# One division for logits and outputs, no rests behind batch 0's scatters, batch 2 in batch 0's rows, and a new written order

## The chip, the cores and the metric

The kernel runs on one core of a Trainium2 chip. The metric is the device time of one execution in microseconds (us); smaller is better. The engines are TensorE (PE; its weight loads are listed apart as PEld), VectorE (DVE), ScalarE (ACT), GpSimd (POOL) and SyncE (SP, which only starts DMA transfers here). Each takes its own instructions in the order in which they are written.

## What is computed

Attention with a polynomial sketch of the keys and queries, then a layer of eight experts of which every token goes to one. B = 4, H = 4, S = 1088, D = 32, R = 8; 4352 tokens of 128 elements, E = 8, F = 1024; everything in fp32.

```python
def phi(x):                                    # S1, S2: (8, 32)
    a = np.einsum('rd,bhsd->bhsr', S1, x)
    b = np.einsum('rd,bhsd->bhsr', S2, x)
    return np.einsum('bhsi,bhsj->bhsij', a, b).reshape(*x.shape[:-1], 64)
q_p, k_p = phi(q), phi(k)
kv = np.einsum('bhsf,bhsd->bhfd', k_p, v)
z = np.sum(k_p, axis=2)
num = np.einsum('bhsf,bhfd->bhsd', q_p, kv)
den = np.einsum('bhsf,bhf->bhs', q_p, z)[..., None] + 1e-06
x = (num / den).transpose(0, 2, 1, 3).reshape(4352, 128)

logits = x @ w_gate                            # (4352, 8)
expert_idx = np.argmax(logits, axis=1)
probs = softmax(logits)                        # with 1e-9 added to the sum
for e in range(8):
    mask = expert_idx == e
    out[mask] = probs[mask, e, None] * (np.maximum(x[mask] @ w1[e], 0) @ w2[e])
```

## The kernel before

The schedule is written by hand. Every piece of work is a named operation (`@op(name)`), and `ORDER`, a table of some 1,100 names, says in which order they are emitted. An engine's queue is what of this list falls to it, so that an operation that waits holds back all that stands behind it on its engine. Buffers are taken from rings and given back in the same order.

**Attention.** Names are `k{b}{c}` and `q{b}{c}` for batch b and half c (512 tokens), `kr{r}` and `qr{r}` for what is left over of two batches (64 tokens each, handled as one batch). `L.*` are loads on SP. PE transposes the inputs (`.t`), ACT copies them out of the matmul banks (`.x`), PE applies the sketch (`.a`), ACT copies one factor (`.l`), DVE forms the products (`.s`, `.o`: L442, L455, 128x1024 elements). For keys PE then adds up kv (`.v`); `e{b}.*` finish it. For queries each half again has two turns: PE transposes phi(q) (`.T`, `.U`; L566), ACT copies it (`.c`, `.d`), PE forms the numerators, the denominator and, by a folded gate matrix, the logits of each head in one product (`.n`, `.N`; L584). ACT adds 1e-6 to the denominators (`.p`, L596), DVE inverts them (`.e`, L600), multiplies the logits (`.g`, L604, into `lgh`) and the outputs (`.y`, L611, into a buffer of the ring `flat`), and ACT copies the outputs with their 16-bit halves apart into the token rows `x_rows` (`.f`, L617). A trailing 2 marks the second turn.

**Routing.** `r{b}` on a batch: DVE adds the heads' logits and takes the greatest (`.a`), ACT the exponentials (`.x`), DVE the one-hot `oh` of the expert (`.b`, L667 to L672) and the gate's weight (`.c`), PE ranks the tokens of each expert (`.p`, L686 and L688), DVE turns ranks into row numbers `row_i` (`.d`, L695 to L701), and POOL scatters the token tiles, 128 tokens each, to their experts' rows in DRAM (`.s{u}`, L707: eight for even and nine for odd batches). Behind every scatter stands `breathe()`, which issues by turns no and two small memsets of `fill` (L632). A token's own number stands in the last word of its row; POOL writes these numbers once per batch (`number_rows`, L236).

**Experts.** The rows are worked on in tiles of 128 tokens of one expert: `j0` to `j9` once batches 0 and 1 are scattered, `j10` to `j17` after batch 2, `j18` to `j26` after batch 3, and the split tiles `j27` to `j37` of twice 64 tokens with two experts (`j34` on lie in conditional blocks `m0`, `m1`; of the four, two are executed). `t0` to `t3` are DVE's tables of which tile belongs to which expert. Per tile: SP loads the rows transposed (`.l`, L897, and the gate with the token number, L899; split tiles take rows, `xr`, and transpose on PE, L948), ACT undoes the 16-bit interleaving (`.c`, L958), DVE copies the expert's w1 out of the eight into `wide` (`.w`, `.W`, L966), PE multiplies by w1 in two halves (`.u`, `.U`; L980, split L984), ACT and DVE apply the maximum with 0 (`.r` into hTa on ACT, L1004; `.q` into hTb on ACT for `j0` to `j9`, L1011, else on DVE, L1013), PE multiplies by w2 (`.d`; L1025, split L1029), ACT scales by the gate (`.y`, L1042), and POOL scatters the rows to the output (`.s`, L1047, with `breathe()` behind). `.X` is ACT's copy of w2 for split tiles (L973).

The first load of a group waits for all scatters of the batches that it needs:

```python
                for b in range(min(g + 2, B)):
                    for i in scattered[b]:
                        tc.add_manual_dep(d.ins, i.name, landed, reason="rows of the tile")
```

Of the kernel before, what the change touches and what calls it, by code (L numbers as in the profile page):

```python
# [13 lines left out]
U16 = mybir.dt.uint16  # L14
# [8 lines left out]
warm L.q0 k00.t k00.x S.t L.q1 k01.t S.m k01.x k00.a k01.a L.k1 k00.l k00.s kr0.t kr0.x L.v1 k00.o kr0.a k00.v  # L23
k01.l k01.s kr0.l k01.o q01.t kr0.s q00.t q01.x k01.v e0.s kr0.o e0.r q00.x q11.t C.late e0.k L.qr0 q00.a L.fill
q00.l q11.x e1.s C.later L.x7 q01.a q00.s q00.o q01.l L.kr1 e0.t q01.s q01.o e0.m e0.z k10.t L.k2 q11.a L.k3
k10.x q10.t k11.t k10.a q10.x q01.U q11.l q11.s q00.T k11.x qr0.t q10.a q11.o e0.c k11.a k10.l L.q2 k10.s qr0.x
k10.o q00.c k11.l D0 k11.s q01.d q00.U q00.d q01.T k11.o qr0.a L.qr1 q00.n q00.N q10.l q10.s q00.p L.x0 q01.N
q01.c q01.n q00.p2 q00.e q00.e2 q00.y2 q00.f2 q01.p q00.y L.vr1 k10.v qr0.l k11.v q01.e q01.p2 q01.g q10.o
q01.e2 e1.r qr0.s k20.t e1.k q00.g q01.g2 kr1.t qr0.o q00.g2 r0.a r0.b k31.t q10.U q10.T k20.x k30.t kr1.x r0.x
q10.d qr0.T L.q3 qr0.c k20.a r0.p r0.c k31.x k30.x r0.d q11.U q01.y k20.l kr1.a q11.d k20.s e1.t q00.f e1.c e1.m  # L30
k21.t r0.s2 e1.z q01.y2 kr1.l kr1.s q11.T r0.s1 q01.f k31.a q11.N q01.f2 r0.s4 qr0.n k21.x k20.o qr0.p L.v2 L.w7
r0.s0 kr1.o q10.N q11.p2 qr0.e qr0.y k31.l k30.a k31.s k21.a q10.p2 qr0.g k30.l q10.e2 q11.c q11.e2 k20.v q10.y2
# [40 lines left out]
def kernel(  # L73
# [12 lines left out]
    nc = tc.nc  # L86
# [66 lines left out]
    flat_bufs = ring("flat", 3, [128, 2, DM])  # L153
# [987 lines left out]
```

## Time and profile before

| what | value |
|---|---|
| median of three runs | 214.54 us (213.92 to 215.52) |
| profiled execution | 212.96 us, of which the span of the engines is 211.2 us |
| granted clock of TensorE, mean | 0.974 of full |
| PE busy | 191.7 us, 91% of the span |
| DVE, ACT, POOL busy | 126.4, 104.2, 95.1 us |
| bytes moved by DMA | 23.22 MB, mean 110 GB/s |

Line numbers (L617) are those of the kernel before. A row of a group gives line, engine, operation, output and inputs with their shapes, the count, and behind the bars the busy us, the mean ns of one, and how long the engine sat idle just before and what ended most of it. A row of a timeline gives start, duration, instruction and count; in brackets, the idle time before it and what released it ("issue": nothing that the trace shows). A "q" behind an engine's name means its sequencer. A row of the chain is a piece of the work that ended last, followed back from the end. In all of them, the releaser is inferred from the semaphore that came last.

### The profile page before, as it was taken

Reading aid. Unit: us, or ns where it says so; the run is one execution under the profiler, and the core shown is the slowest. Engines: PE = TensorE matmul, PEld = TensorE weight load, DVE = VectorE, ACT = ScalarE, POOL = GpSimd, SP = SyncE. Lnnn points to the kernel's source line nnn. Section 1 sums busy time; section 2 is a strip of 40 time slices with the busy share of each in tenths; the row PEclk is TensorE's granted clock in tenths of the full one; section 3 lists DMA queues with packets and bytes.
Section 4 is the critical chain, followed back from the end, with each engine's and each line's share of the span. In section 5 each row is a group of like instructions: output and inputs, shape, how many; then the busy total and the mean of one; then the engine's idle time right before and its main releaser. Section 6 shows DMA issues by size and latency. Waiting matters only on the chain.

```text
span 211.2 us, 7499 instructions
## 1 busy us (share of the span) xinstructions
PE 191.7 (91%) x2749; PEld 185.8 (88%) x2749; DVE 126.4 (60%) x403; ACT 104.2 (49%) x257; POOL 95.1 (45%) x176
## 2 busy tenths in 40 slices
PE   7899989989953999999989899999999999999940
PEld 7799989779853999999989799999999999999940
DVE  6699888998987858889137381614334914235200
ACT  2356667647733557555526466532325295634310
POOL 5010006768762875268400746703502007776762
PEclk9999999999995899999999999999999999999995
DMA  4998999999411243123211223212200001010100
GB/s 149 291 325 247 274 326 388 320 370 354 127 43 38 53 73 56 39 66 75 56 38 33 60 55 85 54 43 42 70 3 14 6 5 35 33 34 32 40 17 26
DMA packets 35709, 23.22 MB, mean 110 GB/s; under 512 B 17138, under 2 KB 33396, under 8 KB 35672
## 3 DMA queue, kind: packets, MB, share of 16 engines
q1 hardware_dynamic: 32824, 17.95, 30.9%
q0 software_dynamic: 2304, 4.50, 6.6%
q8 instruction: 24, 0.39, 0.9%
q10 hardware_dynamic: 544, 0.26, 0.4%
q14 instruction: 13, 0.11, 0.2%
HBM read 15.84 MB, written 5.35 MB: 100 GB/s over the span
## 4 chain that ended last, share of the span: by engine, by line
PE 74%; POOL 6%; DMA 5%; issue 5%; SPq 4%; ACT 4%; DVE 1%; POOLq 0%; ACTq 0%
PE bank L1025 19%; PE bank L980 19%; PE bank L984 7%; PE bank L427 7%; PE bank L1029 6%; PE bank L410 4%; POOL out_dram L1047 3%; DMA xr<-xs_dram 3%; PE bank L584 3%; PE bank L464 2%; PE bank L566 2%; SPq L899 2%; PE bank L254 2%; POOL xs_dram L707 2%; SPq L885 1%
## 5 line engine op out<-in xcount | busy, mean ns | idle before, releaser
L980 PE MATMUL bank<-xgT,wide 128*128 128x128 f32 x432 | 53.0, 281 | 4.9 <-ACT den_q L596 4.8
L980 PEld LDWEIGHTS bank<-xgT,wide 128*128 128x128 f32 x432 | 51.4, 197 | 5.3 <-ACT den_q L596 4.9
L707 POOL DMA_INDIRECT xs_dram<-x_rows,row_i x34 | 36.1, 1062 | 36.2 <-ACT x_rows L617 19.8
L1013 DVE TENSOR_SCALAR hTb<-bank 128x512 f32<-128x512 f32 x26 | 17.9, 689 | 49.2 <-PE bank L980 24.8
L1047 POOL DMA_INDIRECT out_dram<-y,xg x27 | 26.8, 993 | 34.7 <-ACT y L1042 24.4
L966 DVE COPY wide<-w_all 128x1024 f32 x49 | 32.9, 710 | 3.6 <-issue 3.5
L1004 ACT ACTIVATE hTa<-bank 128x512 f32<-128x512 f32 x36 | 21.3, 595 | 26.3 <-PE bank L984 8.6
L1025 PE MATMUL bank<-w_all,hTa 128*128 x216 | 28.8, 277 | 0.3 <-DVE low L850 0.2
L1025 PE MATMUL bank<-w_all,hTb 128*128 x216 | 28.6, 276 | 0.0
L1025 PEld LDWEIGHTS bank<-w_all,hTa 128*128 128x128 f32 x216 | 26.3, 192 | 0.7 <-DVE low L850 0.4
L1025 PEld LDWEIGHTS bank<-w_all,hTb 128*128 128x128 f32 x216 | 26.3, 192 | 0.0
L1047 POOL DMA_INDIRECT out_dram<-y,to x11 | 11.2, 1016 | 24.1 <-ACT y L1042 11.0
L455 DVE TENSOR_TENSOR wide<-sum 128x1024 f32<-128x1024 f32 (+1 forms) x18 | 20.3, 1133 | 0.3
L632 POOL MEMSET fill<- 1x130 f32 x72 | 17.5, 243 | 2.1
L427 PE MATMUL bank<-s_cat,xT 128*128 128x128 f32 x136 | 18.1, 280 | 0.4 <-ACT xT L420 0.4
L984 PE MATMUL bank<-xgT,wide 128*64 128x64 f32 x576 | 17.7, 222 | 0.0
L984 PEld LDWEIGHTS bank<-xgT,wide 128*64 128x64 f32 x576 | 17.3, 138 | 0.2
L427 PEld LDWEIGHTS bank<-s_cat,xT 128*128 128x128 f32 x136 | 16.3, 192 | 1.0 <-ACT xT L420 0.6
L1042 ACT ACTIVATE y<-bank,xg 128x128 f32<-128x128 f32 x27 | 9.3, 363 | 14.5 <-PE bank L1025 14.5
L958 ACT COPY xgT<-turned 128x256 uint16<-128x256 uint16 x27 | 12.3, 477 | 7.5 <-DMA turned<-xs_dram 7.4
L420 ACT COPY xT<-bank 128x512 f32<-128x512 f32 (+2 forms) x20 | 9.7, 505 | 8.0 <-DVE xT L419 3.7
L617 ACT COPY x_rows<-flat 128x512 uint16<-128x512 uint16 (+1 forms) x18 | 10.6, 595 | 4.4 <-DVE flat L611 4.3
(178 smaller groups left out, 293.4 us busy)
## 6 DMA issues: line engine op xcount, KB each, us to landing
w_all<-in_moe_w_dram SPq DMA_DIRECT2D x16, 512.0 KB
wide<-in_v_dram SPq DMA_DIRECT2D x4, 512.0 KB
wide<-in_q_dram SPq DMA_DIRECT2D x4, 512.0 KB
wide<-in_k_dram SPq DMA_DIRECT2D x3, 512.0 KB
xr<-xs_dram SPq DMA_DIRECT2D x22, 32.5 KB
xs_dram<-x_rows,row_i POOLq DMA_INDIRECT x34, 3.1
xs_dram<-x_rows SPq DMA_DIRECT2D x1, 520.0 KB
turned<-xs_dram SPq DMA_TRANSPOSE x27
```

The costliest lines, as they stand in the source:

```text
L427: nc.tensor.matmul(t[:, ts(i, 128)], lhsT=st["xT"][:, ts(i, 128)], rhs=s_cat.rearrange("p w t g r -> p (w t g r)"), start=True, stop=True)
L455: nc.vector.tensor_tensor(dst, a[:, :, :, None].broadcast_to([128, n * 4, R, R]), b[:, :, None, :].broadcast_to([128, n * 4, R, R]), ALU.mult)
L632: nc.gpsimd.memset(fill[0:1], 0.0)
L707: d = nc.gpsimd.indirect_dma_start(out=xs_dram[:], out_offset=bass.IndirectOffsetOnAxis(ap=st["row"][:, u:u + 1], axis=0), in_=x_rows[b][: ...
L966: nc.vector.tensor_copy(out=s["w1", i], in_=w1_all[:, ds(r, F)])
L980: nc.tensor.matmul(t[:, ts(c, 128)], lhsT=s["w1", 0][:, w], rhs=s["xT"], start=True, stop=True)
L984: nc.tensor.matmul(t[ts(g, 64), ds(c * 128 + i * 64, 64)], lhsT=s["w1", i][:, ds((c0 + c) * 128 + g * 64, 64)], rhs=s["xT"][:, ts(i, 64)], ...
L1004: nc.scalar.activation(s["hTa"], s["ha"], AF.Relu)
L1013: nc.vector.tensor_scalar(s["hTb"], s["hb"], 0.0, None, ALU.max)
L1025: nc.tensor.matmul(t[:, :DM], lhsT=h[:, ts(c % 4, 128)], rhs=w2_all[:, ds(r + c * DM, DM)], start=(c == 0), stop=(c == 7))
L1029: nc.tensor.matmul(t[ts(i, 64), :DM], lhsT=h[:, ds(c % 4 * 128 + i * 64, 64)], rhs=s["w2"][:, ts(c, DM)] if i else w2_all[:, ds(r + c * DM ...
L1047: d = nc.gpsimd.indirect_dma_start(out=out[:], out_offset=bass.IndirectOffsetOnAxis(ap=s["xg"][:, 1:2].bitcast(I32), axis=0), in_=s["y"], ...
```

## The change

1. `.g` and `.y` become one DVE instruction. It multiplies 40 elements per head (8 of the logits, 32 of the outputs) into `heads_of`, 128x320 elements for a turn; ACT's copy `.f` reads the outputs from there, and routing sums the logits from there. `flat` is gone, and the bank is given back after one use.
2. `breathe()` issues nothing behind batch 0's scatters; the turns of the other scatters stay what they were.
3. Batch 2 has no token rows of its own: it takes those of batch 0, and POOL writes batch 2's token numbers into them in a new operation `N2`, between the scatters of batch 1 and 2.
4. `ORDER` is another table.

```diff
@@
     for b in range(B):
-        t = last_rows if b == B - 1 else new(f"x_rows{b}", [128, J + 1, XW])
+        t = last_rows if b == B - 1 else x_rows[0] if b == 2 else new(f"x_rows{b}", [128, J + b % 2, XW])
         x_rows.append(t)
-        lgh.append(lgh[b - 2] if b > 1 else new(f"lgh{b}", [128, J + 1, H * E]))
-        if b < B - 1:
+        heads_of.append(heads_of[b - 2] if b > 1 else new(f"heads_of{b}", [128, J + b % 2, H, XC]))
+        if b < 2:
             number_rows(b)
...
+    @op("N2")
+    def _():
+        number_rows(2)
...
-                nd = u["nd"] = banks.take(2)
+                nd = u["nd"] = banks.take()
...
-            @op(x + ".g" + a)
-            def _():
-                nc.vector.tensor_tensor(dst(i0, m)[1].rearrange("p j (h e) -> p j h e", h=H), ndv()[:, :, :, 0:E],
-                                        u["den"][:, :, :, None].broadcast_to([128, m, H, E]), ALU.mult)
+            @op(x + ".y" + a)
+            def _():
+                nc.vector.tensor_tensor(dst(i0, m)[1], ndv()[:, :, :, 0:XC],
+                                        u["den"][:, :, :, None].broadcast_to([128, m, H, XC]), ALU.mult)
                 banks.give(u["nd"])
-            @op(x + ".y" + a)
-            def _():
-                xf = u["flat"] = flat_bufs.take()
-                nc.vector.tensor_tensor(xf[:, 0:m].rearrange("p j (h d) -> p j h d", h=H), ndv()[:, :, :, E:XC],
-                                        u["den"][:, :, :, None].broadcast_to([128, m, H, D]), ALU.mult)
-                banks.give(u["nd"])
             @op(x + ".f" + a)
             def _():
-                nc.scalar.copy(out=dst(i0, m)[0].bitcast(U16).rearrange("p j (w c) -> p j w c", w=2),
-                               in_=u["flat"][:, 0:m].bitcast(U16).rearrange("p j (c w) -> p j w c", w=2))
-                flat_bufs.give(u["flat"])
+                rows, of = dst(i0, m)
+                nc.scalar.copy(out=rows.bitcast(U16).rearrange("p j (w h d) -> p j w h d", w=2, h=H),
+                               in_=of[:, :, :, E:XC].bitcast(U16).rearrange("p j h (d w) -> p j w h d", w=2))
...
-    def breathe():
+    def breathe(b=None):
+        if b == 0:
+            return
         for _ in range(next(turns)):
             nc.gpsimd.memset(fill[0:1], 0.0)
...
-            nc.vector.tensor_reduce(lgs, lgh[b][:, :n].rearrange("p u (h e) -> p u e h", h=H), AX.X, ALU.add)
+            nc.vector.tensor_reduce(lgs, heads_of[b][:, :n, :, 0:E].rearrange("p u h e -> p u e h"), AX.X, ALU.add)
...
-                breathe()
+                breathe(b)
```

What the table moves shows on the engines' queues. The loads on SP now begin k0, v0, the leftovers of k and v, the gate, q0, k1, q1, then w2 of expert 0, the fill of the token rows in DRAM, v1, q2, the leftover queries, w2 of expert 2, w1 of expert 1, k3, k2, w2 of expert 4, q3; of the experts' weights, only w2 of 7 and of 0 stood ahead of q3 before.

POOL, where batch 0's scatters (first line) are followed by batch 1's, before (names carry the buffer's number):

```order
L707 DMA xs_dram<-x_rows_230,row_i_686 39168x130 x2
L632 MEMSET fill 1x130 x2
...
L707 DMA xs_dram<-x_rows_230,row_i_686 39168x130 x2
L632 MEMSET fill 1x130 x2
L707 DMA xs_dram<-x_rows_233,row_i_945 39168x130 x2
L632 MEMSET fill 1x130 x2
```

and now:

```order
L705 DMA xs_dram<-x_rows_227,row_i_648 39168x130 x8
L705 DMA xs_dram<-x_rows_230,row_i_844 39168x130 x2
L630 MEMSET fill 1x130 x2
...
L705 DMA xs_dram<-x_rows_230,row_i_844 39168x130
L237 IOTA x_rows_227 128x8
L705 DMA xs_dram<-x_rows_227,row_i_1348 39168x130
L630 MEMSET fill 1x130 x2
```

The eight scatters of batch 0 stand in a row, and an iota for N2 stands between batch 1's last scatter and batch 2's first.

PE, at the end of attention, where the rank matmuls of batch 2 (`upper`, `ones_b`) and the first expert tile (xgT with wide) follow the last numerators (kvx with q_pT), before:

```order
L584 MATMUL bank_67<-kvx_204,q_pT_93 64x82 x8
L584 MATMUL bank_65<-kvx_204,q_pT_95 64x82 x8
L584 MATMUL bank_72<-kvx_204,q_pT_94 64x82 x8
L686 LDWEIGHTS upper
L686 MATMUL bank_70<-oh_1282,upper 128x64
L688 LDWEIGHTS ones_b
L688 MATMUL bank_70<-oh_1282,ones_b 128x64
...
L584 MATMUL bank_69<-kvx_204,q_pT_93 64x82 x8
L980 MATMUL bank_71<-xgT_130,wide_79 128x128 x4
```

and now, with the leftover's transposition (L569) among them:

```order
L587 MATMUL bank_72<-kvx_201,q_pT_94 64x82 x8
L569 MATMUL bank_65<-ident,wide_84 128x128 x2
L587 MATMUL bank_69<-kvx_201,q_pT_95 64x82 x8
...
L587 MATMUL bank_70<-kvx_201,q_pT_93 64x82 x8
L684 LDWEIGHTS upper
L684 MATMUL bank_66<-oh_1252,upper 128x64
L686 LDWEIGHTS ones_b
L686 MATMUL bank_66<-oh_1252,ones_b 128x64
...
L978 MATMUL bank_71<-xgT_127,wide_78 128x128 x4
```

The rank matmuls have moved behind all numerators, directly ahead of the first expert tile, which is now j4.

DVE, up to the one-hot `oh` of batch 2 that the rank matmuls need, before:

```order
L611 TENSOR_TENSOR flat_98<-bank_65,den_q_1129 128x256
L604 TENSOR_TENSOR lgh_231<-bank_71,den_q_1156 128x64
...
L604 TENSOR_TENSOR lgh_231<-bank_65,den_q_1129 128x64
L604 TENSOR_TENSOR lgh_231<-bank_70,den_q_1189 128x64
L604 TENSOR_TENSOR lgh_231<-bank_66,den_q_1206 128x64
L653 TENSOR_REDUCE lgs_626<-lgh_231 128x64
...
L667 SCALAR_TENSOR_TENSOR cand_632<-sh_630,rev 128x64
L670 TENSOR_REDUCE first_1280<-cand_632 128x8
L672 TENSOR_TENSOR oh_1282<-cand_632,first_1280 128x64
...
L966 COPY wide_79<-w_all 128x1024
L611 TENSOR_TENSOR flat_100<-bank_71,den_q_1156 128x256
```

and now:

```order
L964 COPY wide_78<-w_all 128x1024
L607 TENSOR_TENSOR heads_of_228<-bank_72,den_q_1128 128x320
...
L964 COPY wide_79<-w_all 128x1024
L603 RECIPROCAL den_q_1148<-den_q_1148 128x8
...
L607 TENSOR_TENSOR heads_of_228<-bank_68,den_q_1148 128x320
...
L458 TENSOR_TENSOR wide_84<-sum_91 128x256
...
L964 COPY wide_75<-w_all 128x1024
L651 TENSOR_REDUCE lgs_560<-heads_of_228 128x64
...
L668 TENSOR_REDUCE first_1250<-cand_570 128x8
L670 TENSOR_TENSOR oh_1252<-cand_570,first_1250 128x64
```

Three copies of an expert's w1 (w_all to wide) that stood behind `oh` stand ahead of it, among merged divisions.

The tiles of the first group run in the order j4, j0, j7, j1, j2, j9, j5, j8, j3, j6 (before: j0, j2, j5, j8, j1, j3, j9, j4, j7, j6), and all three drains of POOL (`D0` to `D2`) stand behind batch 3's scatters, where before one stood early in batch 1's keys, one behind the first loads of tiles, and one among the split tiles' preparations. The first transposition of a split tile (`.b`, L948) comes behind the products of more whole tiles: j10, j12, j16, j15, j11 and j24 are multiplied by w1 ahead of it, and j10, j11, j12 and j16 by w2; before, only j14, j16 and half of j17, by w1.

More of the change, by code (lines that the diff above doesn't have):

```diff
@@ L22 @@
 ORDER = """
[L23 to L32, printed above, removed]
@@ L63 @@
[L63 to L66 removed]
+k00.t L.q0 k00.x S.t k01.t S.m k01.x L.k1 k00.a k00.l k00.s k01.a L.q1 k00.o k01.l k01.s warm kr0.t k01.o L.x0
@@ new lines @@
+kr0.x kr0.a kr0.l kr0.s kr0.o e0.s k00.v q00.t q01.t k01.v e0.r q00.x L.fill q01.x C.late q00.a C.later q11.t
+q00.l q00.s e0.k q01.a q10.t q11.x q00.o q01.l q01.s q11.a e0.t q10.x k10.t q01.o q10.a q11.l k11.t q11.s k10.x
+q01.U e0.m k10.a q10.l k11.x q01.d q11.o e0.c q10.s q00.T k11.a q00.U k10.l e0.z q10.o k10.s q00.c q01.T k10.o
+k11.l q00.d q00.n e1.s q01.c q01.N L.v1 L.q2 k11.s q00.p q00.N k11.o q01.p2 L.qr0 L.x2 q01.n q00.e q01.e2 q21.t
+q00.p2 q00.y q11.T q00.e2 q01.y2 q01.p q01.e q00.y2 q01.y r0.a q11.c L.vr1 qr0.t r0.b k10.v qr0.x q00.f2 k11.v
@@ new lines @@
+j4.w q20.f r1.s7 q31.U q21.y j0.w r1.s4 q20.e2 e3.k e3.t e3.m e3.c qr1.l e3.z q20.y2 qr1.s q30.N qr1.o q20.f2
+j2.w q30.n qr1.T q31.d q31.N q31.c qr1.c qr1.n r2.a j4.l j4.c r2.b j7.l q31.n j5.w j0.l qr1.p j7.w r2.x r2.p
+qr1.e j4.u j4.U q31.p j4.r q31.e j7.c j1.w j1.l j4.q q31.p2 j4.d j2.l j7.u q31.y q30.p2 q30.p j0.c j4.y r2.d
+q30.e r2.c j1.c q21.f q30.e2 N2 j0.u j9.w q30.y j0.r j7.r j0.U j7.U q31.e2 r2.s2 q21.f2 q31.y2 j2.c t0.d j7.q
+j1.U q31.f2 j1.q r2.s3 t1.a q30.y2 j1.u j7.d j0.q j2.U j2.q r2.s0 j9.l qr1.y r2.s7 j5.l j1.r j2.u r2.s5 t1.d
@@ new lines @@
+j36.b j36.c j25.l j15.y j37.b j20.l j37.X j35.l j24.r j13.u j13.r j13.U j13.q j26.w j14.U j24.d j14.r j18.w j8.s
+j22.u j21.c j22.U j19.c j28.l j37.o j13.d j25.w j16.s j35.L j35.j j36.W j14.q j32.l j17.U j32.L j31.y j22.r
+j13.y j17.u j14.d j26.l j6.s j26.c j17.r j21.w j21.U j21.u j14.y j37.W j34.X j23.w j28.L j32.o j15.s j28.j j9.s
+j28.o j22.q j26.u j17.q j26.U j18.l j33.j j20.c j11.s j22.d j37.c j26.r j23.l j26.q j10.s j37.w j26.d j33.b
+j22.y j14.s j35.b j24.y j19.U j21.r j23.c j21.q j32.j j20.u j29.y j23.u j19.u j19.q j17.d j20.U j33.X j23.r
@@ L67 @@
+j28.u j21.s j32.U j32.r j28.r j28.U j28.q j30.u j30.U j30.X j30.r j30.q j26.s j34.s j27.u j32.X j30.o j28.d
+j28.y j33.q j30.d j23.s j28.s j27.r j27.q j30.y j33.r j30.s j32.q j32.d j32.y j32.s j33.d j27.d j33.y j33.s
+j27.y j27.s
 """
@@ L152 @@
     kvz_bufs = ring("kvz", 2, [128, 96])
-    flat_bufs = ring("flat", 3, [128, 2, DM])
     turned_bufs = ring("turned", 5, [128, 2, 128], U16)
@@ L233 @@
     nc.gpsimd.iota(last_rows[:, 0:J, DM + 1].bitcast(I32), pattern=[[0, J]], base=ABSENT, channel_multiplier=0)
-    x_rows, lgh = [], []
+    x_rows, heads_of = [], []
     def number_rows(b):
@@ L624, in rows_of @@
     def rows_of(b, j0):
-        return lambda i, m: (x_rows[b][:, ds(j0 + i, m), 0:DM], lgh[b][:, ds(j0 + i, m)])
+        return lambda i, m: (x_rows[b][:, ds(j0 + i, m), 0:DM], heads_of[b][:, ds(j0 + i, m)])
     turns = itertools.cycle(RESTS)
-    def breathe():
+    def breathe(b=None):
+        if b == 0:
+            return
         for _ in range(next(turns)):
```

59 lines of the change are left out of this document (25 added, 34 removed).

## The prediction

> **What bounds the kernel now.** I read the forty slices of the page first. A digit is the busy share of a slice of 5.28 us; PEclk is the clock that the throttle granted TensorE.
>
> ```profile
> PE   7899989989953999999989899999999999999940
> POOL 5010006768762875268400746703502007776762
> PEclk9999999999995899999999999999999999999995
> ```
>
> TensorE (PE) is the wall: 9 in nearly every slice. What can be won without removing matmuls are the holes: slices 12 and 13 (where the clock falls too), 9-and-8 patches, and the end. I then asked for the chain of waits around the first hole (start, duration, what) and for PE's timeline there (start, duration, instructions, and in brackets the idle time before them).
>
> ```profile
> 61.62 2.31 DMA xs_dram<-x_rows,row_i
> 63.95 2.42 DMA turned<-xs_dram
> 66.39 0.48 ACT xgT L958
> 72.44 1.79 PE bank L980 x16
> 61.05 0.19 PE L686 MATMUL bank<-oh,upper 128*128 128x64 bf16 x1 [1.00 <-DVE oh L672]
> 61.07 0.35 PE L688 MATMUL bank<-oh,ones_b 128*128 128x64 bf16 x8
> 61.35 0.79 PE L584 MATMUL bank<-kvx,q_pT 128*64 128x82 f32 x16
> 66.92 3.67 PE L980 MATMUL bank<-xgT,wide 128*128 128x128 f32 x16 [4.78 <-ACT den_q L596]
> ```
>
> The last attention matmul ends at 61.35 + 0.79 = 62.14; the first expert matmul starts at 66.92. The chain tells what it waits for: batch 1's last scatter (61.62), its landing, the transposed load of tile 0, ACT's copy. The name in PE's bracket (den_q) was done long before; the chain is the better witness. Then the clock, by windows (span, busy us of PE, PE's weight loads, DVE, ACT, POOL, granted clock, DMA share, GB/s):
>
> ```profile
> 60.10:63.50 3.40, 1.10 (x25) 0.91 (x24) 2.70 (x12) 0.68 (x5) 1.91 (x4) 1.00 0.14 43
> 63.50:66.90 3.40, 0.00 (x0) 0.00 (x0) 2.14 (x11) 1.34 (x5) 0.04 (x1) 0.50 0.11 20
> 66.90:70.30 3.40, 3.38 (x16) 3.38 (x17) 3.03 (x10) 1.10 (x3) 2.41 (x5) 0.50 0.21 45
> ```
>
> The clock is 0.50 from about 63.5 to 70.3, so the first tile's 16 matmuls take 3.67 us where the next tile's take 1.79.
>
> **The change, part by part.** Every time is against the profiled execution: 212.96 us, of which 211.2 are the span and 1.76 lie around it.
>
> *1. POOL, the scatters of batches 0 and 1.*
>
> ```profile
> 32.61 1.16 POOL L707 DMA_INDIRECT xs_dram<-x_rows,row_i  x1 [13.64 <-ACT x_rows L617]
> 43.75 0.97 POOL L707 DMA_INDIRECT xs_dram<-x_rows,row_i  x1 [0.55 <-ACT s_rem L502]
> 45.03 0.97 POOL L707 DMA_INDIRECT xs_dram<-x_rows,row_i  x1 [0.30 <-issue]
> 47.44 1.27 POOL L707 DMA_INDIRECT xs_dram<-x_rows,row_i  x1 [1.01 <-DVE wide L455]
> ```
>
> Two scatters without a rest stand 45.03 - 43.75 = 1.28 apart. Batch 0's eight took from 32.61 to 47.44, 14.83 us; four pairs with a rest at 3.3 each (6., below) are 13.2, so 1.6 went on long ones. Back to back they need 8 x 1.28 = 10.2 us, and with the same 1.6 for long ones 11.8: batch 1's first may start at 44.4, 3.0 earlier. Its own rests stay. Its last moves from 61.62 to 58.6 if rows and indices are there (bounds 58.6 and 61.6). Landing, load and copy as above (2.31 + 2.42 + 0.48, with 0.05 to PE) put the first tile at 63.9. So POOL is no longer alone in what the hole waits for.
>
> *2. What the first expert matmul waits for instead.* Routing's rank matmuls of batch 2 (r2.p) now stand directly ahead of the first tile's on PE, and need `oh` from DVE.
>
> ```profile
> 25.85 0.23 DVE L604 TENSOR_TENSOR lgh<-bank,den_q 128x64 f32<-128x64 f32 x1
> 26.00 1.22 DVE L455 TENSOR_TENSOR wide<-sum 128x1024 f32<-128x1024 f32 x1
> 45.18 0.41 DVE L611 TENSOR_TENSOR flat<-bank,den_q 128x256 f32<-128x256 f32 x1
> 45.51 2.35 DVE L455 TENSOR_TENSOR wide<-sum 128x1024 f32<-128x1024 f32 x2
> 60.77 0.23 DVE L672 TENSOR_TENSOR oh<-cand,first 128x64 bf16<-128x64 f32 x1
> 61.80 0.69 DVE L966 COPY wide<-w_all 128x1024 f32 x1 [0.63 <-issue]
> 62.41 0.75 DVE L611 TENSOR_TENSOR flat<-bank,den_q 128x256 f32<-128x256 f32 x2
> ```
>
> From start to start a division for logits costs 26.00 - 25.85 = 0.15, one for outputs 45.51 - 45.18 = 0.33. The slope from 64 to 256 elements, 0.18/192 = 0.94 ns each, makes 320 elements 0.33 + 0.06 = 0.39: the merger saves 0.09 a pair (between 0.15, if the extra columns ride along, and nothing, if the 40-wide pieces cost). Up to `oh` of batch 2 the order has 13 logit and 11 output divisions before, and 13 merged ones now: 13 x 0.15 + 11 x 0.33 = 5.58 against 13 x 0.39 = 5.07, -0.5. But three weight copies (L966) now stand ahead of it: each 62.41 - 61.80 = 0.61 and up to 0.63 idle before it while the expert's number is read; 0.61 to 1.24, I take 1.05: +3.15 (1.8 to 3.7). `oh` moves from 61.0 to 61.0 - 0.5 + 3.15 = 63.65; rank matmuls 0.30 (61.05 to 61.35); first expert matmul at 63.95 instead of 66.92: **-3.0**. Bounds: 62.1 (PE's own work of before, none of it removed) to 66.9: -4.8 to 0.
>
> [...]
>
> *4. The middle.* The split tiles' loads (xr) queue on SP behind transposing ones. Below stand the window of these 30 us, a row of PE's waits behind the hole (total us, times, longest), and SP's row of the loads.
>
> ```profile
> 100.00:130.00 30.00, 28.11 (x244) 27.14 (x243) 14.03 (x42) 15.15 (x38) 11.32 (x18) 1.00 0.23 52
> PE bank L948 <- ACT xgT L941: 1.5, 2, 0.9
> 106.13 14.18 SPq L899 DMA_DIRECT2D xr<-xs_dram  x14
> ```
>
> PE loses 1.88 of these 30 us, 1.5 of it on the split tiles' rows. In the new order PE has seven more half products by w1 (0.9 each) and four more products by w2 (1.79 each), 13.4 us, between the first expert matmul and the first split tile's transposition, while the loads stand in SP's queue about where they did: **-1.9** (0 to -1.9).
>
> *5. New waits on PE.* The first tile's down product follows its up product with no other tile between: ACT must do half 1, another tile's copy, half 2. (Groups of the page: busy us, mean ns, idle before; then two rows of the chain, split tiles.)
>
> ```profile
> L1004 ACT ACTIVATE hTa<-bank 128x512 f32<-128x512 f32 x36 | 21.3, 595 | 26.3 <-PE bank L984 8.6
> L1013 DVE TENSOR_SCALAR hTb<-bank 128x512 f32<-128x512 f32 x26 | 17.9, 689 | 49.2 <-PE bank L980 24.8
> 153.71 3.88 PE bank L984 x128
> 157.59 3.50 PE bank L1029 x64
> ```
>
> Half 2 is ready 0.60 + 0.48 (the copy in the chain) + 0.60 = 1.68 after half 1's products; PE has the other half of the ups (0.9) under it: **+0.8**. At the end five split downs stand in a row (3.50/2 = 1.75 each) with three hTb buffers, so one half-2 evaluation (0.69) waits for a down to end: about **+0.85** with its way. Both 0 to double.
>
> *6. The end*, from the timelines of ACT and POOL.
>
> ```profile
> 197.90 0.97 POOL L1047 DMA_INDIRECT out_dram<-y,xg  x1 [0.64 <-ACTq L1095]
> 203.13 0.37 ACT L1042 ACTIVATE y<-bank,to 128x128 f32<-128x128 f32 x1 [1.38 <-PE bank L1029]
> 204.51 0.97 POOL L1047 DMA_INDIRECT out_dram<-y,to  x1 [0.61 <-issue]
> 205.79 0.97 POOL L1047 DMA_INDIRECT out_dram<-y,to  x1 [0.30 <-issue]
> ```
>
> POOL's last scatter starts 2.66 us after the last scaling (203.13), because it is behind: two pairs with their rests took 204.51 - 197.90 = 6.61, so 3.3 a pair. In the new order the last twelve scatters stand beside ten split ups (3.88/4 = 0.97 each) and five downs (1.75): 18.5 us of PE work, against five pitches of 3.3 = 16.5 from their first pair to the last. POOL has caught up by then, and the last scatter starts about 0.5 after the last scaling: **-2.2** (0 to -2.2).
>
> *7. Without a price.* Eight memsets less and one wait for a number (N2: POOL numbers batch 0's rows again once its scatters have read them) lie on POOL between batches 1 and 2, where POOL has idle slices (digits 2 and 6); one queue round of it delays only batch 2's scatters, needed about 15 us later. Buffers of x_rows: batch 2's `f` waits for batch 0's last scatter, done by 44 when it is written near 60.
>
> Sum: -3.0 - 1.7 - 1.9 + 0.8 + 0.85 - 2.2 = -7.15. 212.96 becomes 205.8. The median of the three runs shown is 214.54, 1.58 above the profiled one; on it the forecast is **207.4**.
>
> **Rivals.**
>
> *(a) The clock falls all the same, or part of the hole stays.* A window with PE busy 1.10 of 3.40, and 1.4 us of pause at its end, preceded the drop, and the new hole still has PE waiting for DVE around 60 to 64. Term 3 is lost (+1.7), and up to half of 2 (+1.5): 209.1 to 210.6. For it: those rows. [...] Chance 0.20, its time faster still.
>
> *(b) The hole is filled but given back.* If batch 1's last scatter still waits for a late output copy on ACT (19.8 of POOL's 36.2 idle us ahead of scatters were ended by L617), it stays near 61.6, terms 2 and 3 are nil, and the new waits (+1.65) stand against what is left of 4 and 6: 212.1 with both, 216.2 with neither. Chance 0.13.
>
> ```profile
> L707 POOL DMA_INDIRECT xs_dram<-x_rows,row_i x34 | 36.1, 1062 | 36.2 <-ACT x_rows L617 19.8
> 24.00:27.00 3.00, 2.94 (x123) 2.57 (x117) 2.31 (x6) 1.26 (x7) 0.00 (x0) 1.00 0.84 175
> GB/s 149 291 325 247 274 326 388 320 370 354 127 43 38 53 73 56 39 66 75 56 38 33 60 55 85 54 43 42 70 3 14 6 5 35 33 34 32 40 17 26
> ```
>
> *(c) Slower: inputs late.* The new order issues four experts' weights (0.5 MB each) and the fill ahead of the inputs of batches 2 and 3. Added up, batch 3's queries end 8.3 MB down SP's queue. By the GB/s of the slices (six of 5.28 us move 8.5 MB) they land near 31 us, and in PE's new order they are wanted at about 35. At the slowest rate of a window in loading, the 175 above, they land at 8.3/0.175 = 47: 12 us late. Each us of lateness past 35 adds one; from 7 on, the gain is gone, so the turning point is a mean rate below 8.3/42 = 198 GB/s. Against: that rate would have to last all through, with 274 to 388 in the slices around it. Chance 0.09: 215 to 219.
>
> *(d) The change's own parts do nothing:* the merger's 0.5 us of DVE and the removed memsets without a better order: within (b).
>
> **How the numbers follow.** My case 0.58, (a) 0.20, (b) 0.13, (c) 0.09. A measurement of this kernel tells about 1% (2.1 us). Faster by over 1% (under 212.4): all of mine and (a), less 0.01 at its end: 0.77; within 1%: (b), 0.13; slower, (c) and the 0.01: 0.10. The range runs from 204.0, where terms 2 and 5 come out at their good ends (-1.8, -1.65), to 213.8, in the middle of (b). My case alone: 204 to 210.
>
> **What would show it.** Right: the first expert matmul near 64 with the clock at 1.00 through 60 to 72, released by `oh` or the rank matmuls and not by a transposed load; batch 1's last scatter before 59; PE over 9.8 in each ten us of the middle; the last scatter within 1 us of the last scaling. Wrong: a weight load or q transposition on PE waiting for a DMA before 50 us, a second clock of 0.50, a POOL backlog at the end, or PE waits on hTb among the last downs.

## The result, and the profile after

| | kernel before | changed kernel |
|---|---|---|
| median | 214.55 us (213.92 to 215.52, 4 runs) | 206.33 us (206.02 to 208.41, 4 runs) |
| ratio | | 0.963, 95% interval 0.956 to 0.971 |
| profiled execution, its span | 212.96, 211.2 | 208.41, 206.6 |
| granted clock, mean | 0.974 | 0.996 |

A second session gave 206.75 against 213.59: 0.967 (0.961 to 0.973). The forecast was 207.4. The medians are of all executions, while a ratio and its interval leave out those that were over 1.5% above the fastest of their kernel, and where none is given too few were left. One thing has to be kept in mind in all that follows: the profiled execution of before was 1.6 us faster than its median, and that of after 2.1 us slower. By the profiles the change is worth 4.55 us, by the medians 8.2 and 6.8. The experiments ran on three chips, and on two of them the kernel before itself took 220 to 221 us; a run is compared here with the kernel before of its own session only. The changed kernel as it stands ran in two sessions only, and in neither did the kernel before take 220: what the change gains on those two chips is not shown. Variants of it that ran there came to 0.986, 1.000 and 1.018.

The same three rows of the page, after:

```profile
PE   7999989999779999999999999999999799999980
POOL 5010006787760267575615850581441477046762
PEclk9999999999999999999999999999999999999998
```

The hole in slices 12 and 13 (5 and 3 before) has become two slices of 7; a new 7 stands at 165 us; the end is shorter. PE's timeline shows what is left of the hole (one row is ACT's):

```profile
54.55 0.63 PE L467 MATMUL bank<-wide,wide 128*32 128x64 f32 x27
56.56 0.25 PE L467 MATMUL bank<-wide,wide 128*32 128x64 f32 x3 [1.38 <-issue]
60.16 0.36 PE L523 MATMUL bank<-heads,kvz 128*64 128x80 f32 x4 [0.51 <-ACT kvz L516]
61.53 1.36 PE L587 MATMUL bank<-kvx,q_pT 128*64 128x82 f32 x32 [0.82 <-ACT kvx L538]
63.19 1.67 PE L587 MATMUL bank<-kvx,q_pT 128*64 128x82 f32 x40
65.05 0.19 PE L684 MATMUL bank<-oh,upper 128*128 128x64 bf16 x1 [0.19 <-DVE oh L670]
65.10 0.48 ACT L956 COPY xgT<-turned 128x256 uint16<-128x256 uint16 x1 [1.37 <-DMA turned<-xs_dram]
65.63 2.05 PE L978 MATMUL bank<-xgT,wide 128*128 128x128 f32 x16 [0.20 <-ACT den_qr L599]
165.16 2.02 PE L978 MATMUL bank<-xgT,wide 128*128 128x128 f32 x16 [1.55 <-PEq L1093]
```

The one pause of 4.78 us has become five short ones (1.38, 0.51, 0.82, 0.19, 0.20), the first three of them inside attention. The first expert matmul starts at 65.63 instead of 66.92, close behind the numerators (63.19 + 1.67) and the ranks. Its last 0.20 is for the tile's rows: the transposed load released ACT's copy at 65.10, and the copy ended at 65.58. (The name in PE's bracket, den_qr, is not the cause; it was not either in the hole of before.) The one-hot at 64.99, the numerators at 64.86 and the rows at 65.58 all end within 1 us. L1093 in the last row is the end of a conditional block, `m1`, which is not executed; it stands in mid-stream now and stood behind PE's last product before. In PE's own order the tiles of the first group run j4, j7, j0, j1, j2, j9, j5, j8, j3, j6.

The middle, a window of 30 us:

```profile
100.00:130.00 30.00, 30.00 (x390) 29.84 (x390) 18.72 (x61) 13.20 (x32) 13.66 (x22) 1.00 0.23 51
```

The end, from the chain:

```profile
182.26 9.33 PE bank L982 x320
191.59 9.04 PE bank L1027 x160
200.65 0.38 ACT y L1040
201.30 0.97 POOL out_dram L1045
```

PE does not lose a tenth of a microsecond between 100 and 130. The chain of the end holds PE and one step of ACT; POOL's last scatter starts 0.65 behind the last scaling, where before POOL stood in it with a backlog.

One thing in this execution lies far ahead of the hole. Its first 16 products took 3.54 us, where the second profile of the changed kernel (below) has 1.95:

```profile
7.25 3.54 PE L430 MATMUL bank<-s_cat,xT 128*128 128x128 f32 x16
6.90 1.95 PE L430 MATMUL bank<-s_cat,xT 128*128 128x128 f32 x16
```

PE ran at that slower pace up to about 10.6 us here, at a granted clock of 1.00 (window 7.25 to 10.63); in the profiles of six other runs, the kernel before among them, these 16 took 1.95 to 2.05. PE was some 1.9 us late by that (its next pair of products starts at 11.48, against 9.54). The mean granted clock, 0.996, does not show it. So this execution, the slowest of its four, started late, and the second profile is of one 1.0 us above its median: neither shows a median execution.

### The profile page after: what moved, and what is told of

Same layout as the page of the kernel before. It is cut to its first block, busy times and chain, and to the rows that moved or that the text cites. A ratio compares the mean times of both kernels' runs of the same rounds, so it can differ in the third digit from the quotient of the medians.

```text
span 206.6 us, 7478 instructions
## 1 busy us (share of the span) xinstructions
PE 192.4 (93%) x2749; PEld 185.8 (90%) x2749; DVE 126.3 (61%) x385; ACT 102.9 (50%) x257; POOL 96.9 (47%) x168
## 5 line engine op out<-in xcount | busy, mean ns | idle before, releaser
L705 POOL DMA_INDIRECT xs_dram<-x_rows,row_i x34 | 37.7, 1109 | 38.5 <-DVE sum L445 13.3
L978 PEld LDWEIGHTS bank<-xgT,wide 128*128 128x128 f32 x432 | 50.2, 192 | 2.9 <-issue 1.9
L964 DVE COPY wide<-w_all 128x1024 f32 x49 | 33.4, 710 | 18.2 <-PE bank L978 8.4
L1045 POOL DMA_INDIRECT out_dram<-y,xg x27 | 28.2, 1044 | 34.0 <-issue 9.8
L1002 ACT ACTIVATE hTa<-bank 128x512 f32<-128x512 f32 x36 | 20.8, 597 | 17.5 <-PE bank L978 9.4
L430 PE MATMUL bank<-s_cat,xT 128*128 128x128 f32 x136 | 20.2, 295 | 0.5 <-ACT xT L423 0.4
L430 PEld LDWEIGHTS bank<-s_cat,xT 128*128 128x128 f32 x136 | 18.3, 208 | 1.2 <-ACT xT L423 0.9
L630 POOL MEMSET fill<- 1x130 f32 x64 | 16.5, 258 | 1.9
L971 ACT COPY wide<-w_all 128x1024 f32 x11 | 11.5, 1049 | 4.5 <-PEq L1093 2.1
```

The lines of the kernel that those rows point to most:

```text
L430: nc.tensor.matmul(t[:, ts(i, 128)], lhsT=st["xT"][:, ts(i, 128)], rhs=s_cat.rearrange("p w t g r -> p (w t g r)"), start=True, stop=True)
L630: nc.gpsimd.memset(fill[0:1], 0.0)
L705: d = nc.gpsimd.indirect_dma_start(out=xs_dram[:], out_offset=bass.IndirectOffsetOnAxis(ap=st["row"][:, u:u + 1], axis=0), in_=x_rows[b][: ...
L964: nc.vector.tensor_copy(out=s["w1", i], in_=w1_all[:, ds(r, F)])
L978: nc.tensor.matmul(t[:, ts(c, 128)], lhsT=s["w1", 0][:, w], rhs=s["xT"], start=True, stop=True)
L1002: nc.scalar.activation(s["hTa"], s["ha"], AF.Relu)
```

## The experiments

**The changed kernel again, unaltered.**

> The changed kernel once more, unaltered, with a profile of its own: the yardstick for the other runs, and a look at the 1.5 us that PE idled at the conditional block near 165 us in its first profile, an execution of 208.4 us where the three others took 206.0 to 206.4. If that pause belongs to the kernel, it is there again and the time is 208; if it was that execution's, PE has no idle time between 80 and 200 us and the time is 206.

206.75 us (205.5 to 208.3, six runs) against 213.59. The wait at the conditional block near 165 us is there again, and longer (1.94), in an execution of 207.75 us; both profiles have it. And this execution lost its clock once, in attention, from 57.84 to 61.26:

```profile
56.36 0.25 PE L467 MATMUL bank<-wide,wide 128*32 128x64 f32 x3 [2.36 <-issue]
58.77 1.97 PE L569 MATMUL bank<-ident,wide 128*128 128x128 f32 x8
66.03 2.03 PE L978 MATMUL bank<-xgT,wide 128*128 128x128 f32 x16
164.50 2.02 PE L978 MATMUL bank<-xgT,wide 128*128 128x128 f32 x16 [1.94 <-PEq L1093]
```

The pause near 55 us is 2.36 here instead of 1.38, and eight transpositions (L569) behind it take 1.97 instead of 1.09. Still the first expert matmul comes at 66.03 and its tile runs at full pace.

**The edits without the order.** The changed kernel's code with before's table: of the two places of a pair of divisions the merged one takes the earlier, which is the logits' in 13 of 18 turns and the outputs' in the five others; N2 stands behind batch 1's last scatter.

```diff
-... q00.y ... q00.g ... r1.s4 ...          (before's ORDER)
+... q00.y ...           r1.s4 N2 ...       (18 names .g/.y less, the earlier place kept)
```

> The change's own edits (one division, no rests behind batch 0's scatters, batch 2 in batch 0's rows) in the order of before; the merged division stands where the logits' division stood. Theory A (the written order pays, the edits only make room for it): batch 1's last scatter moves some 3 us ahead, since its eight predecessors need 11.8 us instead of 14.8, so the first expert matmul comes near 64 instead of 66.9; but the middle and the end keep their holes (1.9 and 2.0 us): 209 to 212, at most two thirds of the gain of 8.2. Theory B (the edits pay, the order is a rearrangement): 206 to 208. Theory C (the edits alone do nothing): within 1 us of 214.5.

> The change's edits in the order of before, a second time. Theory A (the order pays): the edits alone bring at most 2 us, 212 to 215, since the old order's hole ends with other waits than POOL's. Theory B (the edits pay): 206 to 209. The first expert matmul tells them apart: near 66 or later for A, near 64 for B.

The first gave 226.7 against 220.6 (1.017, 1.006 to 1.028; single times from 222.2 to 229.4), the second 213.03 against 213.59 (0.997, 0.994 to 1.000). In the second:

```profile
62.53 0.19 PE L682 MATMUL bank<-oh,upper 128*128 128x64 bf16 x1 [1.55 <-DVE oh L668]
66.52 3.79 PE L976 MATMUL bank<-xgT,wide 128*128 128x128 f32 x16 [2.89 <-ACT den_q L597]
```

The hole is where it was, 2.89 us and 1.55 ahead of it, and the first tile runs at half pace (3.79). By the times it is theory A: alone, the edits bring 0.6 us on this chip, and no gain on the other; with them fixed, the order brings the rest here, some 3% (0.967 against 0.997). But A's mechanism was wrong: the last scatter came at 60.59, 1 us earlier and not 3, and the first expert matmul at 66.52 and not near 64. The converse, the new order without the edits, was not run.

**The rests put back** behind batch 0's scatters, in the new order.

```diff
     def breathe(b=None):
-        if b == 0:
-            return
         for _ in range(next(turns)):
```

> The changed kernel with the rests behind batch 0's scatters put back (8 memsets). Theory (the rests set when batch 1's last scatter starts, and that sets the first expert tile): four rests of about 0.7 move the last scatter from 58.8 to about 61.6, landing, load and copy as before (2.3 + 2.4 + 0.5) give a first expert matmul at 66.9 instead of 65.6: +1.3 us, and +1.7 more if the clock falls in the wider hole: 207.6 to 209.3. Rival (DVE's path to the one-hot of batch 2 sets it, POOL has room): under 0.5 us.

217.33 against 220.58 (0.986, 0.980 to 0.992), in a session without a run of the changed kernel, so the times decide nothing. The trace shows:

```profile
59.45 0.97 POOL L703 DMA_INDIRECT xs_dram<-x_rows,row_i  x1 [0.55 <-issue]
67.87 0.20 PE L682 MATMUL bank<-oh,upper 128*128 128x64 bf16 x1
68.12 2.03 PE L976 MATMUL bank<-xgT,wide 128*128 128x128 f32 x16
```

With all rests, batch 1's last scatter starts at 59.45, against 58.80 and 57.44 in the two profiles of the changed kernel: 0.65 and 2.0 later, not the 2.8 of the theory. The first load of a tile starts at 61.76 (61.72, 60.36). PE goes from numerators to ranks to the first tile without a wait, but it comes there late in this execution, by a halved clock from 63.71 on, while ACT's copy of the tile's rows ended at 66.48 (65.58 in the first profile). Whether the rests would hold up a PE that is in time is not shown. The rival that POOL has room for them is borne out by half; its other half, that DVE's one-hot sets the first tile, is not: the one-hot ended at 66.57, over 1 us ahead of the ranks.

**Zeros in the hole** of the kernel before, to test what the clock costs by itself.

```diff
+            if b == 2:           # ahead of the rank matmuls; 12 more ahead of j0's first half product
+                for _ in range(4):
+                    nc.tensor.matmul(pr[:, 0:128], lhsT=zeros, rhs=zeros, start=True, stop=True, skip_group_check=True)
```

> The kernel before with 4 and 12 products of zeros put on PE into the hole ahead of the first expert tile (overwritten afterwards, the rest unchanged). Theory (the hole costs twice, its length and a halved clock behind it): PE stays busy to about 65.5, the clock stays at 1.00, the first tile takes 1.8 us instead of 3.7, and the time falls by 1.6 to 1.9 us to about 212.8. Rival (the clock falls all the same, since PE was idle for most of a window; then the products run at half and end near 68): 214.5 to 216.

> The kernel before with products of zeros in the hole, a second time. Theory (a halved clock behind the hole costs by itself): the clock stays at 1.00, the first tile takes 1.8 us, and the time falls by 1.6 to 1.9 us against the kernel before. Rival: no difference of over 0.5 us.

221.69 against 220.58 and 214.30 against 213.59, no gain: 1.002 (0.997 to 1.008) and 1.003 (0.999 to 1.006). In the first trace the zeros did what the theory wants, and the time was lost elsewhere:

```profile
71.03 1.95 PE L986 MATMUL bank<-xgT,wide 128*128 128x128 f32 x16
84.93 2.07 PE L1031 MATMUL bank<-w_all,hTa 128*128 x8 [2.11 <-ACT hTa L1010]
```

The first tile starts without a wait and runs at full pace, but at 84.83 the clock was halved after all, with a wait of 2.11 us there. In the second trace the zeros did not hold it:

```profile
62.47 2.94 PE L982 MATMUL bank<-zeros 128*128 128x128 f32 x24 [0.37 <-DVE flat L611]
68.35 3.48 PE L986 MATMUL bank<-xgT,wide 128*128 128x128 f32 x16 [2.94 <-ACT den_q L596]
```

The zeros ran at full pace to 65.41, but batch 1's last scatter was late in this execution (63.03 instead of 61.62), the hole went on for 2.94 us, and the clock fell behind it, at 68.0. The granted clocks say more than this one trace: the twelve executions beside this trace lie at 0.978 to 0.993, those of the kernel before, on the same chip, at 0.954 to 0.976, and the time is no better. So in the old order a clock kept better did not shorten the time by anything measurable. Whether that is because the zeros cost what the clock gave, or because the old order has other waits to use it up, is open.

**No rests at the end** of the kernel before.

```diff
-            breathe()
+            if x not in LATE:    # the twelve last output scatters
+                breathe()
```

> The kernel before without rests behind the last twelve output scatters. Theory (POOL's backlog sets the end, 2.66 us behind the last scaling): six rests of about 0.7 are more than the backlog, the last scatter starts within 0.7 us of the last scaling: -2.0, to about 212.5. Rival (the end is set by landing and closing, or scatters without rests are slower by what the rests took): under 0.7 us either way.

> The kernel before without rests behind its last twelve output scatters, a second time. Theory (POOL's backlog sets the end): the last scatter starts within 0.7 us of the last scaling instead of 2.66, and the time falls by 1.5 to 2.0 us. Rival (the scatters wait for their own data, or go slower without rests): under 0.5 us.

227.3 against 220.6 in the first session, without a ratio, so that nothing follows from it; and 224.3 against 220.6 in the second (1.018, 1.010 to 1.027): no gain, and rather a loss of just under 2%. In the second, the mechanism is as expected and the gain is not:

```profile
217.85 0.37 ACT L1043 ACTIVATE y<-bank,to 128x128 f32<-128x128 f32 x1 [1.60 <-PE bank L1030]
218.49 0.97 POOL L1048 DMA_INDIRECT out_dram<-y,to  x1 [0.99 <-ACT y L1043]
```

The last scatter follows the last scaling by 0.64, yet that scaling itself is late: among the last split ups PE pauses five times without a data wait (1.8 us together), waits 1.59 for hTa, and the clock is halved from 211.83 to 215.24. In the first session there is a trace to compare with on the same chip, that of the kernel with zeros, whose end is the old one with its rests. PE's waits from 185 to 225 us (total, times, longest), first with the rests, then two rows without them:

```profile
PE bank L990 <- issue: 0.7, 2, 0.3
PE bank L985 <- issue: 2.2, 4, 1.1
PE bank L1026 <- ACT hTa L1005: 1.7, 1, 1.7
```

In these two executions, then, PE's pauses went along with the missing rests. Why, and whether always, stays open.

**Two divisions again**, in the new order.

```diff
+                for lo, hi in ((0, E), (E, XC)):
-                    (one product over 0:XC)
+                    nc.vector.tensor_tensor(dst(i0, m)[1][:, :, :, lo:hi], ndv()[:, :, :, lo:hi], ...)
```

> The changed kernel with each merged division made as two again (8 and 32 columns of each head, one behind the other in the same place; all else unaltered). By the sum 13 divisions stand ahead of the one-hot of batch 2, each saving 0.09 us: the one-hot and the first expert matmul come 0.5 to 1.2 us later, and the time rises by as much, to 206.8 to 207.5. Rival (DVE's time does not reach the end, since PE's own work is as late): under 0.3 us.

208.45 against 213.59 (0.974, 0.968 to 0.979), 1.7 us above the changed kernel of the same session (0.967, 0.961 to 0.973); the intervals overlap. DVE's rows, each up to the next instruction, and the first tile; first with two divisions:

```profile
24.87 0.56 DVE L608 TENSOR_TENSOR heads_of<-bank,den_q 128x64 f32<-128x64 f32 x2
25.34 0.19 DVE L603 RECIPROCAL den_q<-den_q 128x8 f32<-128x8 f32 x1
67.47 2.03 PE L979 MATMUL bank<-xgT,wide 128*128 128x128 f32 x16
```

and DVE's in the changed kernel's first profile:

```profile
26.13 0.49 DVE L607 TENSOR_TENSOR heads_of<-bank,den_q 128x320 f32<-128x320 f32 x1
26.54 0.19 DVE L603 RECIPROCAL den_q<-den_q 128x8 f32<-128x8 f32 x1
```

0.47 against 0.41: 0.06 each, 0.8 for the thirteen. The first expert matmul came 1.44 later than in the changed kernel's profile of that session (67.47, 66.03). That can't be laid to the divisions: the profiled execution was the slowest of its six (210.86), with pauses of 2.47 and 0.60 us on PE and a halved clock from 57.04 to 60.46. The row gives the price of one division; what thirteen of them cost in time is not shown beyond the overlapping intervals.

**Weights behind the inputs**, and **two weight copies behind the one-hot**, in the new order.

```diff
-L.x0 ... L.x2 ... L.w1 ... L.x4 ... L.q3 ...
+... L.q3 L.x0 L.x2 L.w1 L.x4 ...
```

> The changed kernel with the four weight loads that stand ahead of batch 3's queries (w2 of 0, 2 and 4, w1 of 1) moved behind them on SP; nothing else. Theory (inputs come in time either way): within 0.5 us of the changed kernel. Rival c of the prediction (weights ahead delay the inputs): 1 us or more faster, with fewer waits of PE and ACT in the first 50 us.

```diff
-j4.w ... j0.w ... j2.w ... r2.b ... j5.w j7.w
+j4.w ... r2.b ... j5.w j7.w j0.w j2.w
```

> The changed kernel with two of the three weight copies that DVE makes ahead of batch 2's one-hot (for the tiles j0 and j2) moved behind it. Theory (DVE's path to the one-hot, and to the last kv sums, sets the first expert matmul): each copy costs 0.61, the first expert matmul comes 0.7 to 1.2 us earlier, near 64.6 instead of 65.6 to 66.0, and the time falls by 0.5 to 1.2 us. Rival (the copies only fill time in which DVE waits, or the third tile then waits for its weights): within 0.3 us.

220.31 (1.000, 0.995 to 1.005) and 222.68, both against 220.63, again without a run of the changed kernel beside them: the comparisons that the expectations ask for can't be made, and the second run has no ratio even so. That the inputs come late, the third rival, is settled by the changed kernel's own first profile. The only time before 50 us that PE waits there for an input is this, and the second profile has none:

```profile
5.01 1.08 PE L413 MATMUL bank<-ident,wide 128*128 128x128 f32 x4 [0.15 <-DMA wide<-in_k_dram]
```

Of the copies the trace of the second run says this:

```profile
71.33 0.20 PE L682 MATMUL bank<-oh,upper 128*128 128x64 bf16 x1
```

The one-hot is not waited for (0.19 in the changed kernel): it ended at 70.78, the tile's rows were copied at 70.78 too, and PE came last, with the first tile at 71.58. PE was that late by two pauses without a data wait, 2.25 and 2.61 us, near 40 and 45 us, and a halved clock for 6.8 us behind them. The trace of weights behind the inputs has such a pair as well (2.06, 1.90), and so has the one with the shifted stream below (2.04, 1.94); the two profiles of the changed kernel have none there. All three ran on the chips on which the kernel before takes 220 us. Whether the chip or the edits make these pauses is not known, so the traces say little about what the two edits would do to a PE that is in time.

**The instruction stream shifted.** Small products of zeros at the start instead of three of the eight large ones.

```diff
-WARM = 8
+WARM = 5
+PAD = 43
...
+        for _ in range(n):       # pad(PAD), behind warm(WARM)
+            nc.tensor.matmul(t[0:32, 0:32], lhsT=zeros[:, 0:32], rhs=zeros[:, 0:32], start=True, stop=True, ...)
```

> The changed kernel with 43 small products of zeros (32x32) at its start in place of three of the eight large ones, so that every later instruction of PE stands some 150 places further down its stream while the work stays the same. Theory (the 1.4 to 2.5 us that PE idles among batch 3's key sums near 55 us is a block of instructions that arrives late): the pause leaves its place behind 27 of 32 products; it shows up some 150 instructions earlier, or not at all where the block then has more time, and then the first expert matmul comes 1 to 2 us earlier. Rival (those products wait for data at that place): the pause stays where it was, with the same length.

224.0 against 220.3 (1.018, 1.012 to 1.023; one of the six executions took 392.8 and is not in the ratio). No run of the changed kernel stands beside it on that chip. The padding cost more than planned, 4.29 us for 86 records, so that PE began the real work 2.7 us later:

```profile
31.93 0.25 PE L477 MATMUL bank<-k_rem_p,v_rem 128*32 128x64 f32 x2 [2.36 <-issue]
64.40 0.65 PE L477 MATMUL bank<-wide,wide 128*32 128x64 f32 x32
```

The group of batch 3's key sums that broke off after 27 of its 32 products runs through (64.40, x32), with pauses of at most 0.46 about it, and a long one of the same kind, 2.36, stands in batch 1's key sums. That is what the theory expects, but it does not show the theory: with weights behind the inputs and with two copies behind the one-hot the stream is not shifted, and that group runs through as well (at 60.67 and 61.64), with the long pauses in other places. So the shift need not be what moved the pause, and the first tile did not come earlier. What makes these pauses stays open.

## Why the prediction was right, and where not

The range, the sign and the likeliest case held: 206.33 in 204.0 to 213.8, 207.4 forecast. Step by step, by the two profiles of the changed kernel against that of before, of which the second is from another session:

| step | forecast | first, second profile |
|---|---|---|
| 2. first expert matmul | -3.0 | -1.29, -0.89 |
| 3. first tile at full clock | -1.7 | -1.62, -1.64 (3.67 to 2.05, 2.03) |
| 4. the middle | -1.9 | -1.89, -1.89 |
| 5. new waits: first tiles, last downs | +0.8, +0.85 | about +0.55, 0; +0.29 in both (9.04 for five at 1.75) |
| conditional block in mid-stream | not in the sum | +1.55, +1.94 |
| 6. the end | -2.2 | -2.01, -2.02 |

The rows add up to about -4.4 and -4.2; the second execution gained 1.0 that they do not place. Step 4 came out to a tenth, step 6 to two, and their windows and rows show the mechanism: no PE wait for split rows, no backlog of POOL at the end. In step 5 the wait that was forecast, of the first down products for their second half, is 0.14 of the first profile's 0.55; the other 0.41 is for the next tile's rows. That POOL's backlog alone would have given those 2 us to the kernel before was not borne out by the runs.

**Step 1** had the right result for the wrong reason. Batch 1's last scatter came at 58.80 (forecast 58.6) and 57.44. But with all rests put back it came at 59.45, and without them in the old order at 60.59 instead of 61.62: as far as single executions on different chips can tell, the order has the larger part of the first profile's 2.8 us, and the rests, which were to bring it all, the smaller. And the gain did not reach the tile's rows, which were copied at 65.58, where 63.9 was forecast.

**Step 2** is the one that failed in size: 1.3 and 0.9 instead of 3.0. DVE's pieces were sized well (a copy 0.61, three of them 2.3 with their idle time instead of 3.15; a merged division 0.36 to 0.41), and yet the one-hot was late:

```profile
58.58 0.69 DVE L964 COPY wide<-w_all 128x1024 f32 x1 [0.51 <-DVE heads_of L607]
59.19 0.48 DVE L607 TENSOR_TENSOR heads_of<-bank,den_q 128x320 f32<-128x320 f32 x1
64.77 0.22 DVE L670 TENSOR_TENSOR oh<-cand,first 128x64 bf16<-128x64 f32 x1
```

It ended at 64.99 instead of 63.65. The windows from the start to the end of the one-hot, before and after, tell why (the third busy time is DVE's):

```profile
0.00:61.00 61.00, 56.37 (x975) 52.24 (x976) 52.35 (x176) 35.62 (x105) 25.08 (x64) 1.00 0.89 276
0.00:64.99 64.99, 59.18 (x991) 54.35 (x992) 54.52 (x166) 36.27 (x101) 26.16 (x57) 1.00 0.86 262
```

DVE's work rose by 2.17, near the 2.65 of the sum; the time in which DVE had nothing to do rose from 8.65 to 10.47, by 1.82, and the sum had nothing for that. The other thing it left out is PE: I took its end of attention, 62.14, as it was, "none of it removed", and in the new order PE itself ends at 64.86 and 65.62. In the first profile that went with the slow products at the start (16 in 3.54), a pause of 1.38 and waits of 0.51 and 0.82 on batch 3's kv sums; in the second with a pause of 2.36, the halved clock and one wait of 0.82. The slow start belongs to that execution; the pause behind the same 27 products is in both, and also with two divisions (2.47) and with the rests back (0.59), but not in the three other profiles with the new order. One-hot, PE and the tile's rows arrive within 0.8 us of each other in the first profile, so that making one of them earlier could not have moved the first tile by more than that. The prediction's own sign for step 2, a first matmul "released by `oh` or the rank matmuls and not by a transposed load", is not met there: the last 0.20 us is for the copy of the transposed load.

**Step 3** came out to a tenth, but no run shows what its -1.7 rests on, that a short enough pause leaves the clock at full. The size is half of the 3.4 us from 66.9 to 70.3 that the kernel before ran at 0.50. What the runs showed: at the first tile the granted clock was 1.00 (65.60 to 67.70 in the first profile), behind waits of 0.19 and 0.20, where 4.78 stood before; in the second profile it fell in attention, at 57.84, behind a pause of 2.36 that ended at 56.36; with two divisions it fell at 57.04, in a pause of 2.47 that ended at 57.30; and in the first profile it held behind a pause of 1.38.

**The first rival** (the clock falls all the same) came true in one of the two profiles, at 57.8, not at the hole. It was paid in attention and not at the first tile. **That the edits do nothing without the order** was held to be near no change, and is: -0.6.

The sum, -7.15, is 2.6 and 1.9 more than the profiled executions show (-4.55 and -5.21), and close to what the medians show (-8.2 and -6.8). No profile has the steps of a median execution, so its steps can't be read. The granted clocks give a part of the answer. A fall of 3.4 us to half takes 0.008 off the mean over 206 us (an estimate, half of 3.4 in 206; 0.996 and 0.988 in the two profiles). Of the ten executions of the changed kernel six lie at 0.994 to 0.998, which leaves no room for a whole one; they took 205.5 to 206.4, but for the 208.4 of the one with the late start. The four others lie at 0.985 to 0.990 and took 206.7 to 208.3. So part of the difference may lie in the mishaps of the two profiled executions. Whether step 2 is nearer to its -3.0 without them, or errors cancel, is not known, and until it is, the hit on the median to 1.1 us has to be called luck.

## What to carry to other kernels

When a wait is taken away from the engine that bounds, ask for the second and third wait of that same place before crediting the gain: here the transposed load, the one-hot and PE's own stream ended within 1 us of each other, and 4.8 us of idle time gave 1.3 and 0.9 in the two profiled executions. Edits that free time off the path (fewer instructions, fewer rests, a buffer less) brought next to nothing here until the order used the room (0.3% on one chip); measure them apart from the order, and the order apart from them (the second of these was not run here). An unexecuted conditional block had its price here by where it stood: behind the bounding engine's last product, as in the kernel before, it held up none of PE's work, and in mid-stream PE waited 1.5 to 2.0 us for it in the seven profiles with the new order. And look at more than one profile before pricing a step: each of the two here had a mishap of its own.

## What the runs showed of the hardware

**Ahead of four falls of the clock PE was busy for 30 to 54% of 3.4 us.** In the kernel before the granted clock was 1.00 up to 63.5 us and 0.50 from there to 70.3, for 6.8 us. Three other falls to half lasted 3.4 us: from 57.84 to 61.26 in the changed kernel's second profile, from 57.04 to 60.46 with two divisions, and from 211.83 to 215.24 without rests at the end; the one with two copies behind the one-hot lasted 6.8. The 3.4 us ahead of the fall, in the kernel before:

```profile
60.00:63.40 3.40, 1.14 (x27) 0.97 (x25) 2.70 (x13) 0.68 (x5) 2.01 (x4) 1.00 0.18 54
```

in the changed kernel's second profile:

```profile
54.40:57.80 3.40, 1.44 (x33) 1.18 (x34) 2.86 (x6) 0.39 (x1) 2.49 (x5) 1.00 0.21 65
```

with zeros in the hole (second trace), and without rests at the end:

```profile
64.40:67.80 3.40, 1.01 (x10) 0.82 (x8) 1.17 (x7) 0.00 (x0) 0.86 (x1) 1.00 0.15 39
208.40:211.80 3.40, 1.82 (x33) 1.13 (x27) 0.00 (x0) 0.00 (x0) 2.19 (x3) 1.00 0.07 19
```

and two windows without a fall behind them, around the longest pause of the changed kernel's first profile, and in the first trace with zeros:

```profile
54.40:57.80 3.40, 2.02 (x59) 1.49 (x56) 3.19 (x11) 1.31 (x4) 2.48 (x4) 1.00 0.23 71
132.60:136.00 3.40, 1.53 (x14) 1.34 (x12) 0.69 (x1) 0.01 (x1) 2.26 (x4) 1.00 0.35 81
```

PE was busy 1.14, 1.44, 1.01 and 1.82 of 3.40 ahead of the falls (30 to 54%), and 2.02 and 1.53 (59 and 45%) where it kept its clock. The two groups overlap, so these runs give no busy share at which the clock falls; in none of the four windows ahead of a fall was PE idle throughout.

**A pause of PE without a data wait went with a packet on a DMA queue that the page calls "instruction".** The page lists that queue, q8, with 24 packets and 0.39 MB in the profile of the kernel before and in the first of the changed kernel, some 0.02 MB each; that they carry PE's instructions is inferred from what follows. In a window of 0.1 us such a packet shows in the changed kernel's first profile at 54.0 us (packets, MB, share of 16 engines):

```profile
q8 instruction: 1, 0.02, 64.2%
```

There is one in its second profile at 53.8, one with two divisions at 54.7 and one with the rests back at 55.2. PE went on at 56.56, 56.36, 57.30 and 57.62, some 2.3 to 2.6 us behind the packet each time, and always after the same 27 products (its pauses were 1.38, 2.36, 2.47 and 0.59 us). With the shifted stream a packet at 29.16 stands 2.8 us ahead of the end of the pause at 31.93. Why PE paused behind these packets and not behind others was not tried, and nothing but the order in time ties the pause to the packet.
